# RWKV attention, Sinkhorn gate and eight experts on one core: the gate's products with x streaming past padded weights on four quarters of the array, and Sinkhorn's column sums over tiles by VectorE first

## The chip, the core and the metric

The kernel runs on one NeuronCore of a Trainium2 chip. The metric is the device time of one execution in microseconds (us). The program uses TensorE (matrix products; called PE in the profile, PEld for its weight loads), VectorE (DVE), ScalarE (ACT), GpSimd (POOL) and the DMA queues of SyncE (SP) and POOL. Each engine takes its instructions in the order in which the program gives them; semaphores order the engines against one another.

## The reference

The first half is a linear attention with a decaying state (batch 4, 8 heads, 768 steps, head size 48). Its output, turned into 3072 rows of 384 numbers, is `x`. The second half sends every row through eight experts and weighs their outputs with a matrix `P`, which Sinkhorn normalisation makes from the gate's logits:

```python
logits = x @ w_gate                      # 3072 x 8
P = np.exp(logits - logits.max())
for _ in range(8):
    P /= P.sum(1, keepdims=True) + 1e-09 # rows: over the 8 experts
    P /= P.sum(0, keepdims=True) + 1e-09 # columns: over all 3072 rows
    P *= N / E
for e in range(E):
    out += P[:, e:e+1] * (np.maximum(x @ w1[e], 0) @ w2[e])
```

## The kernel before, in words

The 3072 rows are 24 tiles of 128 (`NTT`). In every tile `x` is held transposed and as the sum of a high and a low fp16 part, in `hbx`: three chunks (`KC`) of 128 columns each, high and low.

**Attention loop.** A loop over `i` from 0 to 26 (`NTT + 3` passes) builds the tiles; tile `i - 2` is transposed by a DMA in pass `i`. Between its steps the loop calls `work(n)`, which emits the next `n` units of expert 0 from the list `units`: a unit `ph` (`g1_unit`) is 9 products into a bank `ph`, which ACT leaves with a Relu to `hb` and DVE then with the low part of the same values, also to `hb` (the DVE row SCALAR_TENSOR_TENSOR `hb<-ph,hb`); a unit `po` (`g2_half`) is 12 products into a bank `po`. There are two banks `ph`, and two of the pool `po`. The units come in groups of seven: ph po ph po ph po ph.

**Gate.** From pass 14 on, each pass also emits `gate_product` for up to two tiles: `x` is the stationary operand (128 columns), the gate's weights stream past it (16 columns, high and low, then 8), six products a tile into a bank `px`. ACT scales the result into `lparts`. In all there are 144 such products and 24 ACT exits.

**Ticks.** After the loop the remaining units are emitted one per tick: `for f in ticks.pop(tick)` runs the tick's small jobs, then `whole(units.pop(0))` emits one unit. The jobs are the last token combinations (`xv`), the weights of the next stage (`wms`, `ws`), and one step of the generator `sinkhorn()` at each of sixteen ticks. A step of Sinkhorn is what stands between two `yield`: a row step (DVE alone) or a column step. Before the change the column step is

```python
T.matmul(pc, ones, pm)          # TensorE: 192 columns, sums over the 128 partitions
V.tensor_reduce(cs, pc)         # DVE: over the 24 tiles
V.tensor_scalar(cs, cs, ...); V.reciprocal(cs, cs); V.tensor_tensor(pm, pm, cs)
```

Six column steps fall in the ticks 7, 12, 17, 22, 27 and 32. In each tick the Sinkhorn step is emitted before the other jobs, and the tick's unit last.

**Stages.** Then fourteen stages follow, one for each half of the experts 1 to 7. `g1_slots` emits slots of three products into banks `bA` to `bC`, `bY`, `bZ`, and after each slot four or five products of the rest of the stage before. The last two column steps stand in slots 5 and 13 of the first stage.

All order comes from the program's text: a product that is emitted ahead of another on TensorE also runs ahead of it.

Of the kernel before, what the change touches and what calls it, by code (L numbers as in the profile page):

```python
# [8 lines left out]
F32 = mybir.dt.float32  # L9
F16 = mybir.dt.float16  # L10
BF16 = mybir.dt.bfloat16
I32 = mybir.dt.int32
AF = mybir.ActivationFunctionType
# [20 lines left out]
def rwkv_sinkhorn_moe(  # L34
# [20 lines left out]
    P = 128  # L55
# [51 lines left out]
    def xpos(p0, n):  # L107
        return part(hbx, F16, p0 * TH * PX, (n * TH, 2 * KC, P)).rearrange("p (o t) c q -> p o c t q", t=TH)
# [4 lines left out]
    def xall(t, lo):  # L113
        return xtile(t)[:, lo * KC : (lo + 1) * KC, :]
# [385 lines left out]
    iswg = const.tile([P, 1], F32, name="iswg")  # L500
    swg = ac.tile([P, 1], F32, name="swg")
    wgm = ac.tile([P, 1], F32, name="wgm")
    wgp = ac.tile([P, KC, 2, E], F16, name="wgp")
    wgh, wgl = wgp[:, :, 0], wgp[:, :, 1]

    wga = ac.tile([P, KC, E], BF16, name="wga")
    gsum = []

    def gate_magnitude():
        S_.activation(wga, wg, AF.Abs, scale=1.0 / 1024)  # L510

    def gate_sums():
        gsum.append(ps2.tile([P, TB], F32, tag="po", name="pcs_g")[:, :E])
# [3 lines left out]
    def gate_split():  # L517
        V.tensor_reduce(wgm, gsum[0], axis=AX.X, op=ALU.max)
        pow2_scale(wgm, iswg, swg, 1.0)
        S_.activation(wgh, wg, AF.Copy, scale=swg)  # L520
        V.scalar_tensor_tensor(wgl, wg, swg, wgh, op0=ALU.mult, op1=ALU.subtract)

    st = {}

# [178 lines left out]
                T.transpose(pt[:, c * P : (c + 1) * P], xs[:, lo, c * P : (c + 1) * P], ident16)  # L703
            S_.copy(xall(tt, lo).rearrange("p c q -> p (c q)"), pt[:, : KC * P])

    gated = [0]

    def gate_product(tt, pg):
        for c in range(KC):
            xh_, xl_ = xall(tt, 0)[:, c, :], xall(tt, 1)[:, c, :]  # L710

            T.matmul(
                pg, xh_, wgp[:, c].rearrange("p l e -> p (l e)"), start=(c == 0), stop=False,
                skip_group_check=True,
            )
            T.matmul(
                pg[:, :E], xl_, wgh[:, c, :], start=False, stop=(c == KC - 1), skip_group_check=True
            )

    def gate_exit(tt, pg):  # L720
        S_.activation(
            lparts[:, tt].rearrange("p l e -> p (l e)"), pg, AF.Copy, scale=inv_s[:, tt : tt + 1]
        )
        del st[tt]


    TS = TB // 2
    xvs = [xv0]
# [89 lines left out]
    def work(n, hold=False):  # L818
        held[0] = hold
        for _ in range(n):  # L820
            if units:
                whole(units.pop(0))
        held[0] = False
# [43 lines left out]
    hooks[12, "early"] = [gate_magnitude]  # L867
    hooks[13, "early"] = [gate_sums]
    hooks[13, "middle"] = [gate_split]

    prep(0)
    load_part(4, "r", r)
# [18 lines left out]
    for i in range(NTT + 3):  # L891
        if i + 2 < NTT and i != TH + 1:
            prep(i + 2)
        if i > NE:
            send_x(i)
        leave(0)
        if i + 1 < NTT:
            bonus_dot(i + 1)
        if i + 1 < NTT and i:
            stage_b(i + 1)  # L900
        if 1 <= i <= NE:
            addends(i - 1)
        if i <= NE:
            send_x(i)
        n = i + 5 if i < 2 else i + 4
        if i != 2 and n < NTT:
            load_part(n, "r", r)
            load_part(n, "k", k)
        if i < 2:
            load_part(i + 3, "v", v)  # L910
        if i == 2:
            Q.dma_start(wg, w_gate.rearrange("(c p) e -> p c e", p=P))
        run(i, "loads")
        if NE <= i < NTT:
            bonus(i)
        leave(1)
        run(i, "early")
        if i > 10:
            work(1)
        if i < NTT:  # L920
            stage_c(i)
        run(i, "masked")
        if 1 <= i <= NTT:
            state_part(i - 1)
            scores_part(i - 1)
        if i == TH + 1:
            turn_x(TH - 1)
        if i < NTT:
            state_product(i)
        if 1 <= i <= NTT:  # L930
            sum_x(i - 1)
        if i < NTT:
            state_sum(i)
        if 1 <= i <= NTT:
            bound_x(i - 1)
        if i > NTT:
            work(2)
        run(i, "middle")
        if 1 <= i and i + 4 < NTT:
            load_part(i + 4, "v", v)  # L940
        for _ in range(n_steps(i)[0]):
            prepare()
        if i > 13:
            bank_ = ps2.tile([P, TB], F32, tag="po", name=f"px_{i}")
            todo = list(range(gated[0], min(gated[0] + 2, i - 2)))
            for n, tt in enumerate(todo):
                gate_product(tt, bank_[:, n * 2 * E : (n + 1) * 2 * E])
            for n, tt in enumerate(todo):
                gate_exit(tt, bank_[:, n * 2 * E : (n + 1) * 2 * E])
            gated[0] += len(todo)  # L950
        if i <= NTT:
            if i > TH:
                work(1 if i == 4 else 3 if i == 10 else 2, hold=i < 10)
            elif i == 0:
                S_.copy(onesb, ones)
                S_.copy(ident16, ident)
        run(i, "end")
        for _ in range(n_steps(i)[1]):
            prepare()
        if i == TH:  # L960
            prep(i + 3)
            scale_x(TH - 1)
            run(i, "last")
            units += [g1_unit(0, fc, 0) for fc in range(FHC)]
            units += [g2_half(0, t, 0, 0) for t in range(TH)]
        done = i - 2
        if TH <= done < NTT and done % TH == TH - 1:
            po_ = done // TH
            for p_, j in ((1, 0), (0, 1), (1, 1)) if po_ == 1 else ((po_, 0), (po_, 1)):
                turn[0] += 1  # L970
                g1 = [g1_unit(p_, fc, turn[0]) for fc in range(j * FHC, (j + 1) * FHC)]
                units += merged(g1, [g2_half(*a_) for a_ in pend])
                pend = [(p_, t, j, turn[0]) for t in range(TH)]
    assert not side and not hooks and not exits[0] and not exits[1]
    att.close()

# [94 lines left out]
    def sinkhorn():  # L1071
# [10 lines left out]
        for it in range(8):  # L1082
            rs = sm.tile([P, NTT], F32, tag="rs", name=f"rs_{it}")
            V.tensor_reduce(rs, pm, axis=AX.X, op=ALU.add)
            V.tensor_scalar_add(rs, rs, 1e-9)
            V.reciprocal(rs, rs)
            V.tensor_tensor(pm, pm, rs.unsqueeze(2).broadcast_to([P, NTT, E]), op=ALU.mult)
            yield
            pc = skp[0].tile([P, NTT, E], F32, tag=skp[1], name=f"pc_{it}")
            T.matmul(  # L1090
                pc.rearrange("p t e -> p (t e)"), ones, pm.rearrange("p t e -> p (t e)"),
                start=True, stop=True,
            )
            cs = sm.tile([P, E], F32, tag="cs", name=f"cs_{it}")
            V.tensor_reduce(cs, pc.rearrange("p t e -> p e t"), axis=AX.X, op=ALU.add)
            V.tensor_scalar(cs, cs, 1e-9, E / NT, op0=ALU.add, op1=ALU.mult)
            V.reciprocal(cs, cs)
            V.tensor_tensor(pm, pm, cs.unsqueeze(1).broadcast_to([P, NTT, E]), op=ALU.mult)
            yield
# [323 lines left out]
```

## Time and profile before

| | before |
|---|---|
| median of 3 runs | 1518.65 us (1518.31 to 1519.0) |
| the profiled execution | 1517.31 us |
| its span in the trace | 1515.8 us |
| TensorE busy | 1499.4 us (99%) |
| DVE, ACT, POOL busy | 1009.2, 675.9, 583.4 us |
| granted TensorE clock | 1.0 |

The difference of 1.5 us between the profiled execution and its span lies around the first and the last instruction. A row of the timeline has the start in us, the time from the first start to the last end of the instructions merged in it, the engine, the operation, the tile written and those read, the shape, the count, and in brackets the idle time of the engine before it with what ended it. Products of TensorE overlap: the end of one lies past the start of the next, so what one of them costs is the distance between starts, and the row of n products of d us each that spans w us has starts (w - d) / (n - 1) apart.

### The profile page before, as it was taken

Reading aid. Unit: us, or ns where it says so; the run is one execution under the profiler, and the core shown is the slowest. Engines: PE = TensorE matmul, PEld = TensorE weight load, DVE = VectorE, ACT = ScalarE, POOL = GpSimd, SP = SyncE. Lnnn points to the kernel's source line nnn. Section 1 sums busy time; section 2 is a strip of 40 time slices with the busy share of each in tenths; the row PEclk is TensorE's granted clock in tenths of the full one; section 3 lists DMA queues with packets and bytes.
Section 4 is the critical chain, followed back from the end, with each engine's and each line's share of the span. In section 5 each row is a group of like instructions: output and inputs, shape, how many; then the busy total and the mean of one; then the engine's idle time right before and its main releaser. Section 6 shows DMA issues by size and latency. Waiting matters only on the chain.

```text
span 1515.8 us, 29018 instructions
## 1 busy us (share of the span) xinstructions
PE 1499.4 (99%) x11734; PEld 849.2 (56%) x11734; DVE 1009.2 (67%) x1678; ACT 675.9 (45%) x1222; POOL 583.4 (38%) x685
## 2 busy tenths in 40 slices
PE   8999999999999999999999999999999999999999
PEld 6667765555555555555555555555555555555555
DVE  7898869576566666666676666666565666566464
ACT  6444435335353544545354544444353544445320
POOL 8779966200224243252424234242424233242200
PEclk9999999999999999999999999999999999999999
DMA  8765522211254666657656676655555455555433
GB/s 180 165 119 116 105 75 88 84 41 61 95 109 55 91 127 92 117 84 131 93 81 116 91 129 92 115 62 96 60 95 57 60 99 57 99 59 96 58 94 131
DMA packets 186441, 143.10 MB, mean 94 GB/s; under 512 B 108737, under 2 KB 180162, under 8 KB 186306
## 3 DMA queue, kind: packets, MB, share of 16 engines
q0 software_dynamic: 44928, 61.36, 32.8%
q1 hardware_dynamic: 141168, 79.87, 20.3%
q8 instruction: 92, 1.51, 0.4%
q14 instruction: 43, 0.35, 0.1%
q10 hardware_dynamic: 210, 0.00, 0.0%
HBM read 55.39 MB, written 80.23 MB: 89 GB/s over the span
## 4 chain that ended last, share of the span: by engine, by line
PE 93%; DVE 3%; issue 1%; ACT 0%; DVEq 0%
PE po L30 49%; PE bZ L30 12%; PE bY L30 12%; PE ph L30 5%; PE bA L30 5%; PE bB L30 5%; PE bC L30 2%; PE py L30 2%; PE pA L30 1%; PE prT L30 0%; PE pkT L30 0%; DVE hb L30 0%; PE px L30 0%; DVE ws L30 0%; DVE tb L30 0%
## 5 line engine op out<-in xcount | busy, mean ns | idle before, releaser
L30 PE MATMUL po<-ws,hbx 128*128 128x384 f16 x3360 | 736.8, 326 | 0.0
L30 POOL DMA_DIRECT2D accd<-stg x288 | 249.8, 868 | 694.5 <-ACT stg L30 676.0
L30 PEld LDWEIGHTS <-hbx 128*128 128x128 f16 x3504 | 333.5, 98 | 293.1 <-issue 1.0
L30 PEld LDWEIGHTS <-ws 128*128 128x128 f16 x3096 | 301.5, 98 | 246.8 <-issue 2.9
L30 ACT ACTIVATE hbx<-tb 128x512 f16<-128x512 f32 x224 | 141.0, 630 | 452.3 <-DVE tb L30 452.3
L30 PE MATMUL po<-ws,hb 128*128 128x384 f16 x1248 | 323.0, 326 | 0.1
L30 DVE TENSOR_TENSOR tb<-bY,tb 128x512 f32<-128x512 f32 x168 | 116.1, 691 | 176.5 <-PE bY L30 176.4
L30 ACT ACTIVATE stg<-po,pe 128x384 f32<-128x384 f32 x312 | 178.8, 573 | 122.3 <-PE po L30 97.9
L30 PE MATMUL bZ<-xv,ws 128*128 128x512 f16 x840 | 227.0, 379 | 0.5 <-DVE tb L30 0.4
L30 PE MATMUL bY<-xv,ws 128*128 128x512 f16 x840 | 227.0, 379 | 0.0
L30 DVE TENSOR_TENSOR tb<-bZ,tb 128x512 f32<-128x512 f32 x168 | 115.6, 688 | 135.8 <-PE bZ L30 135.8
L30 PEld LDWEIGHTS <-hb 128*128 128x128 f16 x1248 | 121.4, 98 | 93.4 <-DVE hb L30 0.4
L30 POOL TENSOR_TENSOR ucb<-rawb 128x256 f32<-128x256 f32 x84 | 75.7, 951 | 119.1 <-DMA rawb<-in_moe_w_dram 119.1
L30 DVE TENSOR_TENSOR tb<-bB,tb 128x512 f32<-128x512 f32 x112 | 77.4, 691 | 49.1 <-PE bB L30 47.2
L30 PE MATMUL ph<-hbx,ws 128*128 128x384 f16 x576 | 104.0, 326 | 1.7 <-DVE hb L30 0.9
L30 DVE SCALAR_TENSOR_TENSOR hb<-tb,hbx 128x512 f16<-128x512 f32 x112 | 77.1, 689 | 24.6 <-ACT hbx L30 19.5
L30 PE MATMUL bA<-xv,ws 128*128 128x512 f16 x336 | 90.8, 379 | 0.0
L30 PE MATMUL bB<-xv,ws 128*128 128x512 f16 x336 | 90.8, 379 | 0.0
L30 DVE SCALAR_TENSOR_TENSOR hbx<-tb,hbx 128x512 f16<-128x512 f32 x112 | 78.1, 698 | 14.7 <-ACT hbx L30 10.4
L30 ACT COPY tb<-bZ 128x512 f32<-128x512 f32 x56 | 32.7, 585 | 65.5 <-PE bZ L30 65.5
L30 DVE SCALAR_TENSOR_TENSOR hb<-ph,hb 128x384 f16<-128x384 f32 x64 | 34.9, 551 | 28.7 <-ACT hb L30 28.4
L30 DVE TENSOR_REDUCE wms<-rawb 128x1 f32<-128x768 f32 x56 | 51.7, 943 | 0.0
(175 smaller groups left out, 1471.5 us busy)
## 6 DMA issues: line engine op xcount, KB each, us to landing
accd<-stg POOLq DMA_DIRECT2D x288, 192.0 KB, 3.7
rawb<-in_moe_w_dram SPq DMA_DIRECT2D x28, 768.0 KB, 7.9
e0d<-stg SPq DMA_DIRECT2D x48, 192.0 KB, 2.0
hb<-e0d SPq DMA_DIRECT2D x48, 192.0 KB, 3.6
vn<-in_v_dram SPq DMA_DIRECT2D x24, 192.0 KB, 3.9
accd<-stg SPq DMA_DIRECT2D x24, 192.0 KB, 1.8
accd<-hb POOLq DMA_DIRECT2D x24, 192.0 KB, 4.8
rawb<-accd SPq DMA_DIRECT2D x24, 192.0 KB, 2.4
```

Of the source, the lines that this page charges most:

```text
L30: return lambda *a, **k: self.tc.keep_in_program_order(f(*a, **k))
```

## The change

**The gate.** `wgp` is padded with zeros to 32 columns (`QP`) for each chunk and part. Now the padded weights are stationary and `x` streams: one product takes three tiles (384 columns) and writes 32 partitions of a bank `pg`; four of them, for four groups of three tiles, write the four quarters of the partitions. Twelve tiles take 24 products. The bank holds the logits turned; ACT copies it to a tile `stg_g` (`gate_products`), and three transposes on TensorE and one multiplication by DVE bring it into `lparts` (`gate_turn`). The first twelve tiles are done in pass 15, the others in pass 26, whose transposes come after two more units `work(2)`; so the ticks begin two units later in the list than before.

**Sinkhorn.** In the column step DVE first sums `pm` over the 24 tiles into `cs` (128 x 8), TensorE then sums `cs` over the partitions (8 columns in place of 192), and DVE reads the result. The steps stand at the same ticks and slots.

```diff
-    wgp = ac.tile([P, KC, 2, E], F16, name="wgp")
-    wgh, wgl = wgp[:, :, 0], wgp[:, :, 1]
+    wgp = ac.tile([P, KC, 2, QP], F16, name="wgp")
+    wgh, wgl = wgp[:, :, 0, :E], wgp[:, :, 0, E : 2 * E]
...
     def gate_magnitude():
         S_.activation(wga, wg, AF.Abs, scale=1.0 / 1024)
+        S_.copy(wgp.rearrange("p c l e -> p (c l e)"), zeros[:, : KC * 2 * QP])
...
         V.scalar_tensor_tensor(wgl, wg, swg, wgh, op0=ALU.mult, op1=ALU.subtract)
+        S_.copy(wgp[:, :, 1, :E], wgh)
...
-    def gate_product(tt, pg):
-        for c in range(KC):
-            xh_, xl_ = xall(tt, 0)[:, c, :], xall(tt, 1)[:, c, :]
-
-            T.matmul(
-                pg, xh_, wgp[:, c].rearrange("p l e -> p (l e)"), start=(c == 0), stop=False,
-                skip_group_check=True,
-            )
-            T.matmul(
-                pg[:, :E], xl_, wgh[:, c, :], start=False, stop=(c == KC - 1), skip_group_check=True
-            )
-
-    def gate_exit(tt, pg):
-        S_.activation(
-            lparts[:, tt].rearrange("p l e -> p (l e)"), pg, AF.Copy, scale=inv_s[:, tt : tt + 1]
-        )
+    GP = P // QP
+    gated = {}
+
+    def gate_products(b):
+        pg = ps2.tile([P, TB], F32, tag="po", name=f"pg_{b}")[:, : TH * P]
+        for c in range(KC):
+            for lo in range(2):
+                for g in range(GP):
+                    T.matmul(
+                        pg[g * QP : (g + 1) * QP].rearrange("p (t q) -> p t q", q=P),
+                        wgp[:, c, lo], xpos(b * GP + g, 1)[:, 0, lo * KC + c],
+                        start=(c + lo == 0), stop=(c + lo == KC), skip_group_check=True,
+                    )
+        gated[b] = stgp.tile([P, DM], F32, tag="stg", name=f"stg_g{b}")
+        S_.copy(gated[b], pg)
+
+    def gate_turn(b):
+        pt = ps2.tile([P, TB], F32, tag="po", name=f"pgT_{b}")[:, : TH * P]
+        for t in range(TH):
+            T.transpose(pt[:, t * P : (t + 1) * P], gated[b][:, t * P : (t + 1) * P], ident)
+        n = GP * TH
+        V.tensor_tensor(lparts ..., pt ..., inv_s ..., op=ALU.mult)
...
+    hooks[15, "middle"] = [lambda: gate_products(0)]
+    hooks[16, "early"] = [lambda: gate_turn(0)]
+    hooks[NTT + 2, "middle"] = [lambda: gate_products(1)]
...
-        if i > 13:
-            bank_ = ps2.tile([P, TB], F32, tag="po", name=f"px_{i}")
-            todo = list(range(gated[0], min(gated[0] + 2, i - 2)))
-            for n, tt in enumerate(todo):
-                gate_product(tt, bank_[:, n * 2 * E : (n + 1) * 2 * E])
-            for n, tt in enumerate(todo):
-                gate_exit(tt, bank_[:, n * 2 * E : (n + 1) * 2 * E])
-            gated[0] += len(todo)
...
+    work(2)
+    gate_turn(1)
...
-            pc = skp[0].tile([P, NTT, E], F32, tag=skp[1], name=f"pc_{it}")
-            T.matmul(
-                pc.rearrange("p t e -> p (t e)"), ones, pm.rearrange("p t e -> p (t e)"),
-                start=True, stop=True,
-            )
             cs = sm.tile([P, E], F32, tag="cs", name=f"cs_{it}")
-            V.tensor_reduce(cs, pc.rearrange("p t e -> p e t"), axis=AX.X, op=ALU.add)
-            V.tensor_scalar(cs, cs, 1e-9, E / NT, op0=ALU.add, op1=ALU.mult)
+            V.tensor_reduce(cs, pm.rearrange("p t e -> p e t"), axis=AX.X, op=ALU.add)
+            pc = skp[0].tile([P, TB], F32, tag=skp[1], name=f"pc_{it}")[:, :E]
+            T.matmul(pc, ones, cs, start=True, stop=True)
+            V.tensor_scalar(cs, pc, 1e-9, E / NT, op0=ALU.add, op1=ALU.mult)
```

Three places in the order of the instructions follow; names carry the tile's number, and what an instruction waits for stands in brackets.

DVE at the second column step (tick 12), before. `xv` is a token combination's low part, `wms` and `wmas` are maxima of the next weights, `hb<-ph` is the low exit of a unit `ph`:

```order
L30 TENSOR_TENSOR xv_4481<-tb,xv_4481 128x3x256 [waits Activation_49]
L30 TENSOR_REDUCE wms_4488<-rawb 128x1
L30 TENSOR_REDUCE wmas_4489<-wms_4488 128x2 [waits DVE_49]
L30 SCALAR_TENSOR_TENSOR hb_73<-ph_3_4721,hb_73 128x384 [waits Activation_49]
L30 TENSOR_REDUCE cs_4735<-pc_4733 128x8 [waits PE_49]
L30 TENSOR_SCALAR cs_4735<-cs_4735 128x8 [waits DVE_49]
```

The same place on DVE in the change:

```order
L30 SCALAR_TENSOR_TENSOR hb_73<-ph_4_4613,hb_73 128x384 [waits Activation_49]
L30 TENSOR_TENSOR xv_4394<-tb,xv_4394 128x3x256 [waits Pool_49]
L30 TENSOR_REDUCE wms_4401<-rawb 128x1
L30 TENSOR_REDUCE wmas_4402<-wms_4401 128x2 [waits DVE_49]
L30 TENSOR_REDUCE cs_4646<-pm 128x8
L30 TENSOR_SCALAR cs_4646<-pc_4648 128x8 [waits PE_49]
```

The sum over tiles keeps its place behind the jobs of the tick before, but it no longer reads `pc`: it makes what `pc` is made from.

TensorE around the column steps 2 to 6 in the change:

```order
L30 MATMUL po_0_4630<-ws_75,hb_73 128x384
L30 MATMUL pc_4648<-cs_4646,ones 128x8 [waits DVE_49]
...
L30 MATMUL ph_7_4733<-hbx,ws_75 128x384
L30 MATMUL pc_4747<-cs_4745,ones 128x8 [waits DVE_49]
...
L30 MATMUL ph_2_4824<-hbx,ws_75 128x384
L30 MATMUL pc_4838<-cs_4836,ones 128x8 [waits DVE_49]
...
L30 MATMUL ph_5_4913<-hbx,ws_75 128x384
L30 MATMUL pc_4927<-cs_4925,ones 128x8 [waits DVE_49]
...
L30 MATMUL ph_0_4993<-hbx,ws_75 128x384
L30 MATMUL pc_5007<-cs_5005,ones 128x8 [waits DVE_49]
```

Before, the product read `pm`, written by DVE in the row step three ticks earlier, and the steps 2 to 5 stood behind a `ph`, 1 and 6 behind a `po`; now 1 and 2 stand behind a `po` and 3 to 6 behind a `ph`, since the ticks begin two units later.

TensorE at the second half of the gate (pass 26 and after it) in the change:

```order
L30 MATMUL po_0_4308<-ws_75,hb_73 128x384
L30 LDWEIGHTS wgp
L30 MATMUL pg_4324<-hbx,wgp 32x384
...
L30 MATMUL ph_5_4351<-hbx,ws_75 128x384
...
L30 MATMUL po_0_4363<-ws_75,hb_73 128x384
L30 MATMUL pgT_4379<-ident,stg_g_4349 128x128 x3
```

The last two groups of `px` before, six products each, stood between the units of the passes 25 and 26; now 24 products `pg` stand in pass 26 in one piece, with one `ph` and one `po` between them and the transposes.

More of the change, by code (lines that the diff above doesn't have):

```diff
@@ L704, in turn_x @@
             S_.copy(xall(tt, lo).rearrange("p c q -> p (c q)"), pt[:, : KC * P])
-    gated = [0]
-    def gate_product(tt, pg):
+    GP = P // QP
+    gated = {}
+    def gate_products(b):
+        pg = ps2.tile([P, TB], F32, tag="po", name=f"pg_{b}")[:, : TH * P]
         for c in range(KC):
-            xh_, xl_ = xall(tt, 0)[:, c, :], xall(tt, 1)[:, c, :]
-            T.matmul(
-                pg, xh_, wgp[:, c].rearrange("p l e -> p (l e)"), start=(c == 0), stop=False,
-                skip_group_check=True,
-            )
-            T.matmul(
-                pg[:, :E], xl_, wgh[:, c, :], start=False, stop=(c == KC - 1), skip_group_check=True
-            )
-    def gate_exit(tt, pg):
-        S_.activation(
-            lparts[:, tt].rearrange("p l e -> p (l e)"), pg, AF.Copy, scale=inv_s[:, tt : tt + 1]
+            for lo in range(2):
[12 more added lines that the diff above has]
+        n = GP * TH
+        V.tensor_tensor(
+            lparts[:, b * n : (b + 1) * n].rearrange("p (g t) l e -> p g t (l e)", t=TH),
+            pt.rearrange("p (t g e) -> p g t e", t=TH, g=GP)[:, :, :, : 2 * E],
+            inv_s[:, b * n : (b + 1) * n].rearrange("p (g t) -> p g t", t=TH)
+            .unsqueeze(3).broadcast_to([P, GP, TH, 2 * E]),
+            op=ALU.mult,
         )
-        del st[tt]
     TS = TB // 2
```

## The prediction

> **What bounds the kernel now.** I read the page first, then TensorE's waits, then the timeline around the gate and around Sinkhorn's column steps.
>
> ```profile
> PE 1499.4 (99%) x11734; PEld 849.2 (56%) x11734; DVE 1009.2 (67%) x1678; ACT 675.9 (45%) x1222; POOL 583.4 (38%) x685
> PE 93%; DVE 3%; issue 1%; ACT 0%; DVEq 0%
> PE py L30 <- ACT rT L30: 2.1, 2, 1.7
> ...
> PE px L30 <- issue: 0.9, 1, 0.9
> ...
> PE bZ L30 <- DVE tb L30: 0.4, 1, 0.4
> ```
>
> The first row is the page's busy time, the second the engines' shares of the chain that ended last, the others are rows of TensorE's waits (total, times, longest). TensorE is busy from end to end and carries 93% of the chain. So a change is worth what it takes out of TensorE's stream, and costs what it makes TensorE wait. A saving on DVE or ACT is worth nothing by itself. But "99% busy" also says that TensorE hardly ever waits for DVE, and that is what the Sinkhorn edit touches.
>
> **The gate's products.** The timeline of TensorE, with the old products between two neighbours, and the transposes of another tile:
>
> ```profile
> 117.06 0.60 PE L30 MATMUL prT<-ident,rp 128*128 128x128 f32 x4
> 117.49 0.60 PE L30 MATMUL pkT<-ident,kp 128*128 128x128 f32 x4
> ...
> 122.16 0.52 PE L30 MATMUL py<-vn,kp 128*32 128x48 f32 x32
> 122.62 0.46 PE L30 MATMUL px<-wgp,hbx 128*128 128x16 f16 x12
> 122.93 2.27 PE L30 MATMUL ph<-hbx,ws 128*128 128x384 f16 x13
> ```
>
> Removed: twelve `px` hold TensorE from 122.62 to 122.93, 0.31 us or 26 ns each; 144 of them cost 3.7 us. One of them also waited 0.9 us (the row of waits above), so at most 4.6 us goes away.
>
> Added: 48 `pg` with 384 streamed columns. Alone, a product of 384 columns has its starts (2.27 - 0.33) / 12 = 0.162 us apart (row `ph`; one takes 0.326). Whether four quarters run at once is seen in `py<-vn,kp`, which also writes 32 columns of the array at a time: its starts are (0.52 - 0.21) / 31 = 10 ns apart (one takes 0.207), four in 0.040 us. A product of 192 fp32 columns has its starts 0.163 apart (the row `pc` x2 further down: 0.49 less 0.326), so 48 columns alone need 0.041. Four quarters thus take the time of one, with two different streams among the four here. I take 12 x 0.162 = 1.95 us; in turn it would be 48 x 0.162 = 7.8.
>
> The Trainium skill (TensorE: Matmul & The Clock Gate, Part 3) gives 3.07 times for four packed tiles in one measurement; by that the twelve rounds would cost an estimated 0.6 us more. The `py` row shows the whole factor of four, and the row decides.
>
> Further: six transposes at (117.49 - 117.06) / 4 = 0.109, 0.65 us, and a change of the array's split ahead of and behind the second half. Ahead of `px` one such change shows: the last `py` starts at 122.47 and would be followed at 122.51; `px` starts at 122.62. So two times 0.1. The first half follows `py` in the same split and needs none more than before. The sum is 1.95 + 0.65 + 0.2 = 2.8 us.
>
> The gain is thus 3.7 - 2.8 = 0.9 us if the 0.9 us of wait turns up elsewhere, 1.8 if it is gone. I take 1.5. The rest of the edit (24 exits of ACT become two copies; one zero fill, one copy, two multiplications of DVE) lies beside TensorE: the transposes come a `ph` and a `po` after the copy, 3.4 us, for one copy of about 0.5 us.
>
> **Sinkhorn's column step.** On TensorE the product of 192 columns gives way to one of 8. The nearest rows are a product with one column, which also waited for DVE:
>
> ```profile
> 226.35 0.20 DVE L30 TENSOR_SCALAR md_gm<-ident,mt_gm 1x1 f32<-1x1 f32 x1
> ...
> 226.66 0.38 PE L30 MATMUL pmax_gm<-md_gm,ones 1*128 1x1 f32 x2
> 226.97 0.82 PE L30 MATMUL ph<-hbx,ws 128*128 128x384 f16 x4
> ```
>
> It holds TensorE 0.31 us, as long as the present `pc` (0.33, from 235.27 to 235.60 below): the fp32 weights `ones` are loaded twice either way. So the smaller product saves nothing. It starts 0.1 us after DVE's end (226.55), which is the price of the hand-over.
>
> On DVE the sum over tiles stays (0.35 us). What changes is who waits. Now TensorE does `pc` in passing, and DVE reads it when it gets there. After the change TensorE must wait until DVE has got there and summed. Behind the waiting `pc` on TensorE stands the whole next unit. So the loss of a step is the time by which DVE's sum lags behind TensorE's arrival. The old rows show that lag, since `cs<-pc` stands at the same place in DVE's order. First the step after tick 7, then the second:
>
> ```profile
> 234.78 0.55 DVE L30 SCALAR_TENSOR_TENSOR hb<-ph,hb 128x384 f16<-128x384 f32 x1
> 235.27 0.49 PE L30 MATMUL pc<-pm,ones 128*128 128x192 f32 x2
> 235.60 1.63 PE L30 MATMUL ph<-hbx,ws 128*128 128x384 f16 x9
> 236.19 0.72 DVE L30 TENSOR_SCALAR cs<-cs 128x8 f32<-128x8 f32 x1
> ...
> 243.88 0.49 PE L30 MATMUL pc<-pm,ones 128*128 128x192 f32 x2
> 245.32 1.62 PE L30 MATMUL ph<-hbx,ws 128*128 128x384 f16 x9 [0.95 <-DVE hb L30]
> 246.78 2.11 PE L30 MATMUL po<-ws,hb 128*128 128x384 f16 x12
> ...
> 247.60 0.16 DVE L30 TENSOR_REDUCE wmas<-wms 128x2 f32<-128x4 f32 x1
> 247.68 0.55 DVE L30 SCALAR_TENSOR_TENSOR hb<-ph,hb 128x384 f16<-128x384 f32 x1
> 248.14 0.35 DVE L30 TENSOR_REDUCE cs<-pc 128x8 f32<-128x192 f32 x1
> ...
> 235.30:249.00 13.70, 12.75 (x79) 7.78 (x79) 12.93 (x22) 5.58 (x11) 13.07 (x17) 1.00 0.13 44
> ```
>
> (The last row is a stretch's busy time: length, PE, PEld, DVE, ACT, POOL.)
>
> Step 1: DVE is free at 235.33, the sum ends at 235.68, TensorE gets it at 235.78 instead of 235.27: 0.5 us.
>
> Step 2: DVE is full here (12.93 of 13.7 us) and gets to its sum 4.3 us after TensorE's `pc`. In the new order DVE has the same work between the two sums, 248.14 - 236.19 = 11.95 us, and TensorE three `ph` (9 x 0.162 = 1.46) and two `po` (12 x 0.162 = 1.95) and the product itself, 8.28 + 0.31 = 8.6 us. DVE starts on its stretch about 0.45 us after TensorE's `pc` begins (hand-over and product). So TensorE waits 0.45 + 11.95 + 0.35 + 0.1 - 8.6 = 4.25 us. Of it, 1.1 us is lost already (245.32 less 243.88 less 0.33, the bracket's wait, for a bank `ph` that DVE gives back). The next unit finds its bank free now, so the step costs 3.15 us more. After it DVE has caught up.
>
> Steps 3 to 6 stand right behind a `ph` in the new order. Then DVE must first bring out that unit's low part, which waits for ACT. The old fifth step shows the chain:
>
> ```profile
> 271.36 0.49 PE L30 MATMUL pc<-pm,ones 128*128 128x192 f32 x2
> 271.56 0.49 ACT L30 ACTIVATE hb<-ph 128x384 f16<-128x384 f32 x1 [0.97 <-PE ph L30]
> 272.08 0.56 DVE L30 SCALAR_TENSOR_TENSOR hb<-ph,hb 128x384 f16<-128x384 f32 x1
> 272.55 0.35 DVE L30 TENSOR_REDUCE cs<-pc 128x8 f32<-128x192 f32 x1
> ```
>
> From TensorE's arrival at 271.36 to the sum's end, 272.90, and 0.1 for the hand-over: 1.64 us, four times, 6.55 us. No other DVE job stands between, so this holds even with DVE idle before.
>
> Steps 7 and 8, in slots 5 and 13 of the first stage:
>
> ```profile
> 296.85 0.49 PE L30 MATMUL pc<-pm,ones 128*128 128x192 f32 x2
> 298.75 0.34 DVE L30 TENSOR_REDUCE cs<-pc 128x8 f32<-128x192 f32 x1
> ...
> 309.47 0.49 PE L30 MATMUL pc<-pm,ones 128*128 128x192 f32 x2
> 312.13 0.35 DVE L30 TENSOR_REDUCE cs<-pc 128x8 f32<-128x192 f32 x1
> ```
>
> By the same sum 299.09 + 0.1 - 296.85 = 2.35 us and 312.48 + 0.1 - 309.47 = 3.1 us. The slots' order does not change, and DVE's work there hangs on TensorE's, so both shift together.
>
> All eight: 0.5 + 3.15 + 6.55 + 2.35 + 3.1 = 15.65 us. Bounds: steps 3 to 6 could cost nothing (then 9.1), and nothing of the rest excludes the whole sum; a gain of TensorE is excluded, because the product costs the same. Little can be won back: behind step 2 TensorE now waits once, 0.4 us (`bZ`, in the rows of waits).
>
> **Sum.** 15.65 - 1.5 = 14.15 us. The profiled execution would go from 1517.31 (span 1515.8 and 1.5 around it) to 1531.5. The median before lies 1.3 us above the profiled execution, so the forecast is 1518.65 + 14.15 = 1532.8 us.
>
> **Rivals.**
>
> *The lag costs only where DVE is truly behind.* If a unit's low exit came out in time in the steps 3 to 6, 9.1 - 1.5 = 7.6 us would be left: 1526.2. Against it stands the order, in which the exit is ahead of the sum.
>
> *The quarters run in turn.* Then the gate costs 5.85 us more: 1538.6. The `py` row speaks against it, though its four quarters share two streams and the new ones have four.
>
> *TensorE's clock falls in the longest wait.* The start of the trace shows TensorE slower after idling:
>
> ```profile
> L30 PE MATMUL pz<-zeros x19: 379/631/631, 1.5 to 9.1; 128*128 128x512 f16 x19
> 1.52 5.92 PE L30 MATMUL pz<-zeros 128*128 128x512 f16 x15 [1.52 <-DVE zeros L30]
> ```
>
> The first fifteen start (5.92 - 0.63) / 14 = 0.378 us apart; at 379 ns each, 0.216 apart as in the full-speed rows of the same shape, they would save 2.3 us. A wait of 4.25 us, in step 2, may bring that once: 1535.1. The longest wait of TensorE now is 1.7 us (the row `py`), so the trace cannot say where it sets in. The Trainium skill (TensorE: Matmul & The Clock Gate, Part 1) says that a whole free-running window of about 3.4 us without work brings half the clock; no run here shows it yet.
>
> *TensorE does not stop.* If it ran the unit behind a waiting `pc`, as it would have to for the edit to be free, only the gate's 1.5 to 1.8 us would be left: 1517.0, on the other side. It decides at the first `pc` that DVE reaches late. Against it: at 245.32 TensorE waited 0.95 us for DVE, with products behind in its queue.
>
> **Chances.** Forecast 0.74, low exit in time 0.08, quarters in turn 0.05, clock 0.05, no stop 0.08. With this measurement about 0.2% (3 us) can be told from no change. Slower by more: the first four cases, 0.92. The last case would be faster by 1.7 us, within 0.2%; with the spread of the gate's gain (up to 4.6 us if the turned products cost nothing) I put 0.04 on faster and 0.04 on the same. The range from 1525.5 to 1538 takes in the smaller loss and the clock, and stops short of the quarters in turn.
>
> **What would show it.** Right: in the timeline each `pc` starts about 0.1 us after the end of `cs<-pm`, and TensorE's waits get a row `pc <- DVE cs` of about 16 us in eight times; `pg` starts in fours 0.162 us apart. Wrong: no such row (TensorE did not stop); `pg` products 0.16 us apart one by one; `ph` products over 0.33 us behind the second step (the clock).

## The result, and the profile after

The changed kernel takes 1534.35 us in the median of five executions (1533.8 to 1537.27), beside 1518.31 us (1516.37 to 1519.0) for the kernel before in the same series. So the change costs 16.0 us by the medians. The ratio, which goes by all executions, is 1.0113, with a 95% interval from 1.01 to 1.0125, or 17.1 us between the means. The forecast was 1532.8, in a range from 1525.5 to 1538.

The profiled execution of the changed kernel took 1535.28 us; its span is 1533.8 and its granted clock 0.997, where it was 1.0 before. The page and TensorE's waits, for comparison with the first fence of the prediction:

```profile
PE 1503.2 (98%) x11644; PEld 848.6 (55%) x11644; DVE 1011.4 (66%) x1680; ACT 672.1 (44%) x1202; POOL 582.3 (38%) x685
PE 94%; DVE 3%; ACT 1%; issue 1%; POOL 1%; ACTq 0%; DVEq 0%; POOLq 0%
PE pc L30 <- DVE cs L30: 13.6, 8, 2.6
PE py L30 <- issue: 6.2, 5, 1.6
...
PE po L30 <- issue: 0.3, 1, 0.3
```

The third row is new. TensorE waits eight times for DVE's sum, 13.6 us in all, and the longest wait is 2.6. It has 90 products fewer than before, and yet 3.8 us more of busy time: a first sign that some products ran slowly. The last two rows, waits that nothing in the trace ends ("issue"), are taken up further down.

**Sinkhorn's steps in the timeline.** Step 2 of the column sums, the one that stands in DVE's densest stretch:

```profile
241.50 0.39 PE L30 MATMUL pc<-cs,ones 128*128 128x8 f32 x2 [0.74 <-DVE cs L30]
241.75 0.97 PE L30 MATMUL ph<-hbx,ws 128*128 128x384 f16 x5
241.93 0.17 DVE L30 TENSOR_SCALAR cs<-pc 128x8 f32<-128x8 f32 x1 [0.48 <-PE pc L30]
...
250.27 0.34 PE L30 MATMUL po<-ws,hb 128*128 128x384 f16 x1 [0.24 <-DVE hb L30]
...
252.62 0.49 DVE L30 TENSOR_REDUCE cs<-pm 128x8 f32<-128x192 f32 x1
253.17 0.39 PE L30 MATMUL pc<-cs,ones 128*128 128x8 f32 x2 [2.56 <-DVE cs L30]
253.41 2.26 PE L30 MATMUL ph<-hbx,ws 128*128 128x384 f16 x9
```

The sum ends at 253.11, and `pc` starts at 253.17. TensorE stands for 2.56 us, with the next `ph` ready behind it. The product itself holds TensorE 0.24 us (253.17 to 253.41); the one of 192 columns held it 0.33. The nine `ph` behind it start (2.26 - 0.33) / 8 = 0.24 us apart instead of 0.162.

A wait in brackets counts from the end of the product before, which comes 0.16 us after the point at which the next one would have started; so each wait costs its bracket and 0.16. By step, for TensorE:

| column step | bracket (us) | cost (us) | forecast |
|---|---|---|---|
| 1 | 0.74 | 0.9 | 0.5 |
| 2, with the 0.24 at 250.27 | 2.56 + 0.24 | 3.1 | 4.25 |
| 3 to 6, each | 1.57 | 1.74 | 1.64 |
| 7 | 2.12 | 2.3 | 2.35 |
| 8 | 1.90 | 2.1 | 3.1 |

Together that is 15.3 before rounding. To be taken off are the waits of before that are gone (1.1 at step 2; 0.44 + 0.16 at a `bZ` 0.64 us ahead of step 8, and 0.2 at an earlier `bZ`, a delay too short for a bracket) and the shorter product (8 x 0.08 = 0.6): about 12.8 us remain.

**The clock.** Busy times of stretches of 3.41 us in the loop and around the steps 2 and 7 (length, PE, PEld, DVE, ACT, POOL, granted clock, DMA share, GB/s):

```profile
49.44:52.85 3.41, 1.61 (x53) 1.25 (x56) 3.31 (x8) 2.66 (x6) 2.44 (x2) 1.00 0.99 267
52.85:56.27 3.42, 3.42 (x123) 2.85 (x116) 3.32 (x9) 1.06 (x1) 2.75 (x3) 0.50 0.95 170
...
247.41:250.83 3.42, 2.96 (x18) 1.46 (x15) 3.42 (x6) 1.25 (x3) 3.34 (x5) 1.00 0.00 0
250.83:254.24 3.41, 1.07 (x8) 0.75 (x9) 2.83 (x7) 1.07 (x2) 3.25 (x5) 1.00 0.17 60
254.24:257.65 3.41, 3.41 (x12) 1.62 (x11) 1.92 (x3) 0.49 (x1) 3.41 (x6) 0.50 0.00 0
257.65:261.07 3.42, 3.42 (x23) 2.06 (x22) 2.60 (x8) 1.91 (x3) 1.80 (x2) 1.00 0.16 57
...
308.86:312.27 3.41, 1.29 (x8) 0.55 (x7) 3.04 (x5) 1.00 (x2) 3.25 (x5) 1.00 0.14 52
312.27:315.68 3.41, 3.41 (x12) 1.57 (x13) 1.33 (x4) 0.00 (x0) 3.41 (x5) 0.50 0.11 41
...
326.00:329.34 3.34, 1.76 (x11) 1.11 (x12) 2.16 (x6) 0.33 (x1) 0.00 (x0) 1.00 0.00 0
```

Behind the steps 2 and 7 the granted clock is 0.50 for one stretch, then full again. In the slow stretch behind step 2 TensorE works on 12 products; in the next one, at full clock, on 23. In the kernel with all sums early (a run further down), which has full clock there, the same units take 1.7 us less. That is so behind both steps, 3.3 us together before rounding. The last row is step 8, whose wait is 1.90 us; the clock is full behind it too (no further stretch of half clock follows).

So the Sinkhorn edit costs 12.8 + 3.3 = 16.1 us in this execution. From the last `py` of the attention loop to the end it takes 16.9 us more than before (209.64 to 1533.79, before 208.53 to 1515.83), so about 0.8 of that is left for the second half of the gate, and 1.1 us lies in the loop. The sum, 18.0, is that of two single executions, one 1.0 us below its median and one 0.9 above.

The clock has a part in that spread. The first two rows show a stretch of half clock in the loop, behind a wait of TensorE for ACT; the profiled execution of the kernel before has none there (its granted clock is 1.0). One such stretch takes 0.5 x 3.41 / 1518 = 0.0011 off the mean clock. In the three series below, the kernel before had a granted clock of 1.0 in 28 executions and of 0.999 in 51 of 83; their medians are 1516.6 and 1518.0 us. The five executions of the change have 0.995 to 0.998.

**The gate.** The two halves:

```profile
131.29 1.28 PE L30 MATMUL pg<-hbx,wgp 128*32 128x384 f16 x24
132.51 1.64 PE L30 MATMUL ph<-hbx,ws 128*128 128x384 f16 x9
...
223.53 1.16 PE L30 MATMUL pg<-hbx,wgp 128*32 128x384 f16 x24
224.62 1.64 PE L30 MATMUL ph<-hbx,ws 128*128 128x384 f16 x9
...
228.04 0.49 PE L30 MATMUL pgT<-ident,stg_g 128*128 128x128 f32 x3
228.37 1.63 PE L30 MATMUL ph<-hbx,ws 128*128 128x384 f16 x9
```

The halves hold TensorE 1.22 and 1.09 us, the three transposes 0.33. That is 2.97 us for both, with the change of the split behind them, against 2.8 forecast and 3.7 for the products that are gone. TensorE's own work became shorter, then, by 0.7 us. But the kernel did not: the next section shows it.

### The profile page after: what moved, and what is told of

Read it like the earlier page. It is cut to its first block, busy times and chain, and to the rows that moved or that the text cites. A ratio compares the mean times of both kernels' runs of the same rounds, so it can differ in the third digit from the quotient of the medians.

```text
span 1533.8 us, 28815 instructions
## 1 busy us (share of the span) xinstructions
PE 1503.2 (98%) x11644; PEld 848.6 (55%) x11644; DVE 1011.4 (66%) x1680; ACT 672.1 (44%) x1202; POOL 582.3 (38%) x685
## 4 chain that ended last, share of the span: by engine, by line
PE 94%; DVE 3%; ACT 1%; issue 1%; POOL 1%; ACTq 0%; DVEq 0%; POOLq 0%
PE po L30 48%; PE bY L30 12%; PE bZ L30 12%; PE ph L30 5%; PE bA L30 5%; PE bB L30 5%; PE py L30 3%; PE bC L30 2%; PE pA L30 1%; DVE hb L30 1%; PE pkT L30 1%; PE prT L30 1%; ACT hb L30 0%; ACT hbx L30 0%; DVE xv L30 0%
## 5 line engine op out<-in xcount | busy, mean ns | idle before, releaser
L30 PEld LDWEIGHTS <-hbx 128*128 128x128 f16 x3360 | 328.8, 98 | 291.2
L30 ACT ACTIVATE hb<-ph 128x384 f16<-128x384 f32 x64 | 31.0, 488 | 65.0 <-PE ph L30 64.4
```

What stands on the lines that cost most here:

```text
L30: return lambda *a, **k: self.tc.keep_in_program_order(f(*a, **k))
```

## The experiments

In each series the kernel before ran on the same chip; its medians there were 1517.67, 1517.72 and 1517.68 us. Times below are medians of 4 to 12 executions, and the code cuts are shortened. One kernel's executions lie up to 5.5 us apart, so intervals are given where it matters.

### Each part alone

The change's gate with the old column step (`e1`):

```diff
+            T.matmul(pc, ones, pm)                 # 192 columns, as before
-            V.tensor_reduce(cs, pm, axis=AX.X)
-            T.matmul(pc, ones, cs)
+            V.tensor_reduce(cs, pc, axis=AX.X)
```

> The gate as in the change, Sinkhorn's column step as before. The forecast's sum says 1.5 us faster than before (0.9 to 1.8). The rival, from the trace of the change, in which the first ph behind the gate's last transposes starts 1.9 us later than before: TensorE's work in the attention loop is not what sets the loop's length, so the products saved there are worth little, and the second half of the gate stands outside of that cover: 0 to 2 us slower. Neither of them gives any row pc <- DVE cs in TensorE's waits.

The old gate with the change's column step, the same edit the other way round (`e2`):

> The gate as before, Sinkhorn's column step as in the change. If TensorE's wait for DVE's sum is the whole cause: 12 to 15 us slower. In this order the steps 2 to 5 stand behind a ph and 1 and 6 behind a po, so step 6 should wait for nothing (about 1.6 us less than in the change) and steps 3, 4, 5 for 1.6 us of idle time each. If the two parts of the change disturb each other (the ticks that begin two units later), it is well under 12 us.

The gate alone took 1519.36 us, a ratio of 1.0014 (1.0005 to 1.0023): it costs 1.7 us, where the prediction had it gain 1.5. Sinkhorn's edit alone took 1530.6 us, 1.0091 (1.0076 to 1.0106), or 12.9 us more. Its waits:

```profile
PE pc L30 <- DVE cs L30: 12.1, 7, 3.0
PE py L30 <- issue: 3.3, 3, 1.5
PE px L30 <- issue: 1.1, 1, 1.1
```

There are seven waits, since the ticks begin two units earlier without the change of the gate and step 6 stands behind a `po`, where its sum is in time. In its profiled execution the clock falls once at the column steps, behind step 7; the longest wait, 2.96 us at step 2, has none behind it. The two parts alone cost 12.9 + 1.7 = 14.6 us; together they cost step 6's 1.74 us as well, since the new gate moves the ticks by two units. That makes 16.3, against 16.0 measured.

### The column steps in pieces

If the loss is TensorE's wait for a sum that DVE makes late, the sum must be made earlier, at the end of the row step ahead of it. This is the change with only that (`e3` all eight, `e5` the second alone, `e6` the third to sixth):

```diff
+            if it in range(8):          # e5: (1,)   e6: (2, 3, 4, 5)
+                V.tensor_reduce(cs, pm, axis=AX.X)
             yield
-            V.tensor_reduce(cs, pm, axis=AX.X)
+            if it not in range(8):
+                V.tensor_reduce(cs, pm, axis=AX.X)
             T.matmul(pc, ones, cs)
```

> The change, but DVE's sum over tiles is issued at the end of the row step, three ticks ahead of the product that reads it. The same instructions on each engine, only this one moved. If the lag of the sum is the cause, all eight waits go, and the time is that of the gate part alone less 0.7 us (the product of 8 columns holds TensorE 0.24 us in the trace, the old one 0.33): 1516 to 1520. If the smaller product itself, or the new read of pc by DVE, cost the time, it stays above 1530.

> The change, with the sum over tiles of the second column step alone issued at the end of its row step. In the trace of the change TensorE lost 3.1 us to this wait (5.08 from the first product of the po ahead to pc, less 1.95), of which the kernel before lost 1.1 too, in another place; and behind it the granted clock was 0.5 for 3.4 us, which cost 1.7 us (ph 2.06 in place of 1.46, po 3.03 in place of 1.95). If the wait brings the slow clock: no stretch of clock 0.5 behind this step, and 3.6 us less than the change, 1530.7. If the slow clock has another cause and comes anyway: 1.9 us less, 1532.4, and the stretch stays.

> The change, with the sums of the column steps 3 to 6 alone issued at the end of their row steps. If each of these waits is the low exit of the ph ahead and the sum behind it (1.74 us each in the trace of the change): 7.0 us less than the change, 1527.4, with the waits of the steps 2, 7 and 8 as they were. If TensorE only waits for something else instead, such as a bank: less than 4 us are won.

| kernel | us | ratio to before | against the change | waits of `pc` for `cs` |
|---|---|---|---|---|
| the change | 1534.35 | 1.0113 | | 13.6 us, 8 times |
| all eight early | 1517.24 | 0.9998 (0.9989 to 1.0007) | -17.1 | none |
| the second early | 1529.98 | 1.0086 (1.0073 to 1.01) | -4.4 | 11.2 us, 7 times |
| the third to sixth early | 1527.32 | 1.0065 (1.0052 to 1.0079) | -7.0 | 7.9 us, 4 times |

The fourth column compares medians of different series; with each kernel taken against the kernel before of its own series, the three differences are 16.5, 3.8 and 6.4 us. With all eight sums early no wait of `pc` is left, and the whole loss is gone. The four middle steps are worth 7.0 us, 4 x 1.74 by the table above. The second is worth 4.4: its wait costs 2.7 us by the table (2.56 and 0.16), and the rest fits the slow stretch behind it, which that kernel doesn't have:

```profile
251.00:255.00 4.00, 4.00 (x27) 2.42 (x25) 3.90 (x9) 2.15 (x5) 3.84 (x5) 1.00 0.14 51
255.00:259.00 4.00, 4.00 (x27) 2.36 (x25) 3.68 (x8) 1.79 (x3) 4.00 (x5) 1.00 0.14 49
...
309.00:313.00 4.00, 4.00 (x23) 2.15 (x22) 2.73 (x5) 1.50 (x3) 3.08 (x5) 1.00 0.02 4
```

The clock is 1.00 where the change had 0.50, with the same work around it. The kernel with the third to sixth early keeps step 2's wait of 2.56 us, and the slow stretch stands behind it again (253.05 to 256.46 us). So the rival "TensorE's clock falls in the longest wait" came true at this step, beside the forecast's own mechanism, as far as single executions show it. But the last row lies behind step 7, which still waits 2.1 us here, and no slow stretch followed it. Not every wait of that length brings one: the 2.96 us of Sinkhorn's edit alone brought none either.

### What the gate's products were worth

The kernel before without its 144 products and 24 exits (`e4`; it leaves the gate out, so that its logits are zero):

```diff
+    V.memset(lparts, 0.0)
-            bank_ = ps2.tile([P, TB], F32, tag="po", name=f"px_{i}")
-                gate_product(tt, bank_[...])
-                gate_exit(tt, bank_[...])
```

> Before, without the gate's 144 products and its 24 exits; the logits are zeros, so P is uniform, and the rest of the computation is unchanged. It shows what TensorE time in the attention loop is worth. If TensorE sets the loop's length: 3.7 us of products and the 0.9 us wait fall away, 4 to 4.6 us faster. If something else sets it: under 2 us faster.

It took 1514.72 us, 0.9986 (0.9977 to 0.9995): 2.1 to 3 us less, where 4.6 had been put down as the most that could go (3.7 of work and 0.9 of wait). The wait of 0.9 us at a `px` is gone, but another stands somewhere else:

```profile
140.30 0.52 PE L30 MATMUL py<-vn,kp 128*32 128x48 f32 x32
140.76 0.50 PE L30 MATMUL po<-ws,hb 128*128 128x384 f16 x2
142.39 0.81 PE L30 MATMUL po<-ws,hb 128*128 128x384 f16 x4 [1.14 <-issue]
```

So that wait didn't belong to the gate's products. Something else makes TensorE stand, and it comes back at another product.

The quarters one after another, in the gate-only kernel (`e7`):

```diff
-        for c in range(KC):
-            for lo in range(2):
-                for g in range(GP):
+        for g in range(GP):
+            for c in range(KC):
+                for lo in range(2):
```

> The kernel with the gate part alone, its 24 products of each half issued one quarter after the other (six for one quarter, then six for the next) in place of four quarters side by side. If the quarters run at once in the change and cannot here: each half holds TensorE 24 x 0.162 = 3.9 us in place of 1.0, and the time rises by 2.9 us if the attention loop covers the first half, by 5.8 us if not: 1522 to 1525. If the quarters never ran at once, nothing changes.

```profile
131.22 2.16 PE L30 MATMUL pg<-hbx,wgp 128*32 128x384 f16 x24
133.31 0.99 PE L30 MATMUL ph<-hbx,ws 128*128 128x384 f16 x5
```

A half then holds TensorE 2.09 us, 0.9 to 1.0 more than in the change's order, and the kernel takes 1520.78 us, 1.0022 (1.0013 to 1.0031), less than was expected of it. 24 products in turn would be 24 x 0.162 = 3.9 us. In the trace the 24 starts can be read as four runs of six, 0.162 us apart within a run, which begin at 131.218, 131.549, 131.891 and 132.232 us. By that reading each quarter begins 0.34 us after the one before, while it still runs, so TensorE overlaps quarters even in this order. The change's order does better: in its second half the last of six rounds starts 1.16 - 0.33 = 0.83 us after the first, five steps of 0.166, so four quarters take the time of one.

### The waits that nothing ends

The "issue" waits of more than 0.2 us in the attention loop were then counted by their place in TensorE's stream: the number of weight loads, products and semaphore instructions ahead of each.

| kernel | start of the waiting product (us) and remainder of its number by 256 |
|---|---|
| before | 32.37: 170; 38.13: 170; 70.67: 171; 106.49: 171; 185.61: 170 |
| the change | 32.62: 170; 38.38: 170; 71.55: 171; 159.96: 170; 178.35: 170; 195.82: 170 |
| the change, all sums early | 31.86: 169; 38.17: 169; 70.73: 169; 158.95: 168; 194.14: 168 |
| before without gate products | 32.12: 169; 38.70: 169; 71.95: 169; 107.56: 169; 142.39: 168 |

All stand at the same place in a block of 256. The part of the page on DMA queues (packets, MB, share) has, for the change:

```profile
q8 instruction: 91, 1.49, 0.4%
```

Each of the 91 packets brings 16384 bytes, and TensorE's 23376 instructions are 91.3 blocks of 256. The transfer behind the wait at 158.95 started at 156.5, that behind 185.61 at 182.9: 2.5 and 2.7 us ahead. A wait appears where TensorE comes to the boundary sooner than that after the transfer's start. This is mostly so where it runs through a block fast, above all in the products `py`, which start 10 ns apart; but the wait at 38.13 ends a block that took 4.7 us without it, since its transfer started only at 35.59. What decides when a transfer starts was not found. The theory is therefore that the next part of the program is late. It says that a shift of the stream moves the waits to other products. Four kernels test it: all sums early, with 36, 68 or 100 small products in place of four large ones ahead of the loop (32, 64 or 96 more, `e9` to `e11`), and the old gate with 64 more (`e12`, from `e8` of the next part):

```diff
-    spin(4)
+    pz16 = ps2.tile([P, TB], F32, tag="po", name="pz16")
+    for _ in range(36):                 # 68, 100
+        T.matmul(pz16[:, : 2 * E], zeros[:, :P], zeros[:, : 2 * E])
```

> This is the change with its sums over tiles early (whose time was 1517.24 us), with 32 products more ahead of the attention loop: 36 products of 16 columns of zeros take the place of four of 512 columns, in a stretch in which TensorE waits 0.76 us for a transfer anyway. Theory (TensorE's code): TensorE waits where a dense run of products crosses a boundary of 256 instructions of its stream, because the next 16 KB of its code come in too late; so far all such waits stand at the instructions 168 to 171 of a 256. With 64 instructions more ahead they go to other products: those at 158.95 (1.15 us) and 194.14 (0.77 us) are gone, new ones stand near 100, 118 or 170 us, at the same remainder of the count. Time: 1516.2 to 1518.2 us, as the new places are about as dense. Rival (the waits belong to what the gate's edit does to the banks or the engines there): the two waits stay at the same products, and the time within 0.5 us of 1517.24.

> The same with 64 products (128 instructions) more. Theory (TensorE's code): the waits at 158.95 and 194.14 are gone, new ones near 126, 144 or 179 us; 1516.2 to 1518.2 us. Rival: the waits stay at the same products, and the time within 0.5 us of 1517.24.

> The same with 96 products (192 instructions) more. Theory (TensorE's code): the waits at 158.95 and 194.14 are gone; the boundaries then fall in the least dense places of the four alignments, near 108, 126 and 178 us, so the waits behind 90 us sum to under 1.2 us instead of 1.9, and the time is 0.5 to 1.5 us lower than with the other alignments: 1515.7 to 1516.7 us. Rival: the waits stay at the same products, and the time within 0.5 us of 1517.24 (or above it by the 0.3 us that the added products may cost).

> The old gate with Sinkhorn's new form and its sums early (whose time was 1515.51 us), with 64 products more ahead of the loop. Theory (TensorE's code): the wait of 0.4 to 0.9 us of a px product at 185.6 us is gone, a new one may stand near 128 or 190 us; the old gate has its time by its alignment as well, so it moves by 0.3 to 1.5 us to either side. Rival (the old gate has no waits by its nature): within 0.3 us of 1515.51.

The place of the wait at 158.95 us, without a shift and with 32 products more:

```profile
157.36 0.43 PE L30 MATMUL py<-vn,kp 128*32 128x48 f32 x22
158.95 0.33 PE L30 MATMUL py<-vn,kp 128*32 128x48 f32 x10 [1.15 <-issue]
159.21 1.64 PE L30 MATMUL ph<-hbx,ws 128*128 128x384 f16 x9
```

```profile
162.28 0.52 PE L30 MATMUL py<-vn,kp 128*32 128x48 f32 x32
162.74 1.64 PE L30 MATMUL ph<-hbx,ws 128*128 128x384 f16 x9
```

The 32 `py` now pass in one piece. In the four shifted kernels the waits stand at other products, a `pg` among them, and again at remainders from 165 to 170 (but for one of 0.2 us at a `pcs` in two of them). With 64 products more, a wait falls into the gate's first half:

```profile
134.11 0.50 PE L30 MATMUL pg<-hbx,wgp 128*32 128x384 f16 x7
136.43 0.97 PE L30 MATMUL pg<-hbx,wgp 128*32 128x384 f16 x17 [1.82 <-issue]
```

| all sums early | us | ratio (95%) | such waits behind 12 us, total |
|---|---|---|---|
| new gate, no shift | 1517.24 | 0.9998 (0.9989 to 1.0007) | 5.9 |
| 32 more | 1516.54 | 0.9989 (0.998 to 0.9998) | 4.8 |
| 64 more | 1520.41 | 1.002 (1.0011 to 1.0029) | 11.1 |
| 96 more | 1517.2 | 0.9999 (0.999 to 1.0008) | 5.8 |
| old gate, no shift | 1515.51 | 0.9984 (0.9975 to 0.9993) | 4.1 |
| old gate, 64 more | 1518.68 | 1.0004 (0.9995 to 1.0013) | 7.8 |

The theory held for where the waits stand. For the times it did less well: with 64 more both kernels became 3.2 us slower, more than was expected, and 96 more, expected as the fastest, was not. Still, the order of the times is that of the waits in the last column within either gate (1517.2 and 1517.24 can't be told apart), and the loop is where they differ: from the last `py` to the end the four kernels with the new gate take 1306.12 to 1306.18 us.

In three pairs that differ in the gate alone (gate alone against before; all sums early; both with 64 more) the new gate is 1.7 us slower by the medians each time; each of these differences is uncertain by about 1 us. In the profiles 0.8 to 1.1 of it lies behind the last `py` (with all sums early 1306.12 us there with the new gate, 1305.14 with the old one): a second half of 24 `pg` and three transposes (1.42 us) stands there in place of 24 `px` (0.62). In the loop TensorE has 1.55 us less to do with the new gate (24 `pg` and three transposes in place of 120 `px`). That work is gone, but the waits for code take it back. From the `py` at 122.42 us of the kernel before, the last one ahead of the gate's first products, to the last `py`:

| kernel | us | waits for code in it | without them |
|---|---|---|---|
| before | 86.11 | 0.9 | 85.2 |
| Sinkhorn's edit alone | 86.38 | 1.1 | 85.3 |
| old gate, all sums early | 86.33 | 0.8 | 85.5 |
| before without gate products | 83.82 | 1.1 | 82.7 |
| gate alone | 86.10 | 2.1 | 84.0 |
| the change | 86.92 | 2.9 | 84.0 |
| new gate, all sums early | 85.96 | 1.9 | 84.0 |

Without the waits the new gate's loop is 1.2 to 1.5 us shorter; with them it is from 0.4 shorter to 0.8 longer. These are single executions. Loop and end together make 0.6 to 1.1 us in the first two pairs' profiles; the rest of the 1.7 us was not located.

### The best version

The old gate with the change's column step and all sums early (`e8`):

```diff
-            T.matmul(pc, ones, pm)                 # 192 columns, behind the yield
+            V.tensor_reduce(cs, pm, axis=AX.X)     # ahead of the yield
             yield
-            V.tensor_reduce(cs, pc, axis=AX.X)
+            T.matmul(pc, ones, cs)                 # 8 columns
```

> The gate as before; Sinkhorn's column step as in the change, but with the sum over tiles issued at the end of the row step. No wait pc <- DVE cs. The product of 8 columns holds TensorE 0.24 us in place of 0.33, eight times, so 0.7 us faster than before if TensorE's time is all that counts here: 1516.5 to 1518. If the early sum on DVE makes the low exits late, 1 to 2 us slower.

It takes 1515.51 us, 0.9984 (0.9975 to 0.9993), 2.2 us less than before and less than both kernels, and more of a gain than the 0.7 us expected. Two column steps, the first and the second:

```profile
235.43 0.28 PE L30 MATMUL pc<-cs,ones 128*128 128x8 f32 x2
235.57 1.14 PE L30 MATMUL ph<-hbx,ws 128*128 128x384 f16 x6
...
243.85 0.28 PE L30 MATMUL pc<-cs,ones 128*128 128x8 f32 x2
244.60 1.62 PE L30 MATMUL ph<-hbx,ws 128*128 128x384 f16 x9 [0.46 <-DVE hb L30]
```

Where the small product did not wait, it holds TensorE only 0.14 us (235.43 to 235.57), not the 0.24 of the change and not 0.33; eight times, that saves 1.5 us. Step 2 also gets shorter, as DVE reads 8 numbers there instead of 192 ahead of the exit that a `ph` waits for: the wait there was 0.95 us and is 0.46 now. Together that is 2.0 us. In the profiles the whole difference lies in this part: from the last `py` to the end this kernel takes 1305.14 us and the kernel before 1307.29, 2.15 more, while the loop is 0.2 us longer. So by these profiles the gain is not one of the code's alignment, though a shift by 64 products costs the same kernel 3.2 us by the medians.

## Why the prediction was right or wrong

**Right: the mechanism and the size of the Sinkhorn loss.** TensorE stops at `pc`, eight times, and waits for DVE's sum. The row foretold as "about 16 us in eight times" reads 13.6 us in eight. Removing the lateness removes 17.1 us (16.5 within its own series), so the rival "TensorE does not stop" falls, and so does "the low exit in time": steps 3 to 6 cost 7.0 us by experiment, against 6.55.

**Mis-sized, in both directions.** Step 2 was put at 4.25 us and took 3.1: DVE's stretch between the two sums was 252.62 - 241.93 = 10.7 us, not the 11.95 of the old order. It held the same jobs, but three of them spanned less: the first operation on `cs` 0.17 instead of 0.72, the multiplication of `pm` 0.36 instead of 0.60, the last `xv` 1.05 instead of 1.52. Step 8 took 2.1 instead of 3.1, and step 1 took 0.9 instead of 0.5. Steps 3 to 6 took 0.1 us more each, because the sum over `pm` takes 0.49 us where the sum over `pc` took 0.35; the forecast had left the duration as it was. "The smaller product saves nothing" was wrong: it holds TensorE 0.24 us instead of 0.33 where it has waited, and 0.14 where it has not, so the row with one column (0.31), which had waited, did not show it. Altogether the waits came out at 12.8 us instead of 15.65.

**A rival that came on top: the clock.** It was given 0.05, for step 2, at 2.3 us. It came twice at the column steps of the profiled execution, behind the steps 2 and 7, and cost 3.3 us. The forecast's own sum was therefore right partly by luck: 2.85 us too much in the waits, 3.3 too little in the clock.

**Wrong: the gate's gain of 1.5 us.** The step that failed is "the gain is thus 3.7 - 2.8 = 0.9 us if the 0.9 us of wait turns up elsewhere, 1.8 if it is gone". The work went about as computed (3.7 less 2.97). The wait does turn up elsewhere, and longer: such waits belong to the place in the program's code and not to the products, as the shifted kernels show, and from 122.42 us to the last `py` they come to 1.9 to 2.9 us with the new gate against 0.8 to 1.1 with the old one. That takes the 1.2 to 1.5 us which the loop does gain. The sum also did not ask where each half stands: the second one stands behind the loop, in place of 24 `px` only, and costs 0.8 us there. So the gate costs 1.7 us by the medians in three pairs, of which 0.6 to 1.1 is accounted for.

**Quarters.** They do run at once, 0.166 us a round in the second half and (1.28 - 0.33) / 5 = 0.19 in the first. The rival "in turn" falls, and even the order that should have shown it costs only 0.9 to 1.0 us a half. The Trainium skill's factor of 3.07 (TensorE: Matmul & The Clock Gate, Part 3) is measured there on four tiles packed by rows, while the quarters here are columns; the 0.6 us more that it gave is not borne out by these two rows.

So the forecast of +14.15 us met +16.0. Sinkhorn's 15.65 was about right (16.1 in the profiled execution; 12.9 + 1.74 = 14.6 by the medians), in other parts than it was made of; the miss is the sign of the gate.

## What to carry to other kernels

Where one engine works in order and is nearly always busy, a step that makes it wait for another engine costs that engine's lag behind it, whatever the step saves; read the lag from the old rows, and move the work that is waited for to an earlier place, which here removed the 16 us of loss, and with the old gate made it a gain of 2. A wait of 2 to 3 us can also bring a stretch of slow clock, 1.7 us here, but does not always. A change of 1 or 2 us in a dense stream is smaller than what a shift of the code alone does, so it needs a comparison over several alignments.

## What the runs showed of the hardware

**The clock falls without a whole idle window.** The stretches of 3.41 us ahead of the two slow ones are not empty: TensorE was busy for 1.07 and 1.29 us of them, and its waits were 2.56 and 2.12 us. The two slow stretches start 58.03 us apart, 17.0 times 3.413, and the one in the loop 201.39 us ahead of the first, 59.0 times, so they lie on one grid. A wait of 1.90 us, whose stretch on that grid (326.00 to 329.34 in the view, but for its first 0.08 us) had 1.76 us of work, brought none. The Trainium skill (TensorE: Matmul & The Clock Gate, Part 1) tells of a free-running window of 3413 ns and of half the clock after an idle one. The grid and the length agree with the trace; that the window must be idle does not, as one with 31%, one with 38% and, in the loop, one with 47% of work were followed by half the clock. Where the limit lies was not measured, and the share of work alone doesn't give it: in the kernel with Sinkhorn's edit alone, 44% ahead of 308.50 brought half the clock, while 45% ahead of 247.06 did not, nor 42% in the kernel with the third to sixth early (the rows below). In the last two cases the wait, of 2.96 and 2.51 us, ran on into the next stretch:

```profile
305.10:308.50 3.40, 1.51 (x10) 0.95 (x11) 2.75 (x6) 1.00 (x2) 3.32 (x6) 1.00 0.16 58
308.50:311.90 3.40, 3.40 (x11) 1.45 (x10) 1.45 (x3) 1.01 (x2) 2.83 (x4) 0.50 0.00 0
...
243.65:247.06 3.41, 1.52 (x10) 0.69 (x7) 3.38 (x6) 1.69 (x3) 3.33 (x4) 1.00 0.16 58
247.06:250.48 3.42, 2.35 (x15) 1.51 (x16) 2.31 (x6) 0.44 (x1) 3.26 (x6) 1.00 0.03 5
...
300.83:304.24 3.41, 1.43 (x8) 0.56 (x6) 3.04 (x5) 1.00 (x2) 3.25 (x5) 1.00 0.24 89
304.24:307.65 3.41, 2.88 (x17) 1.71 (x18) 2.37 (x6) 0.26 (x1) 3.41 (x5) 1.00 0.16 58
```

**Code is waited for.** TensorE stood for 0.2 to 2.8 us at places that lie 256 instructions apart, and went on 2.1 to 3.3 us after the transfer of 16 KB of its program had started. The Trainium skill (Runtime: NRT & Kernel Launch, Instruction fetch mechanics) names blocks of 16 KiB with 256 instructions, fetched while the one before runs, and calls the cost of a crossing mostly hidden. The size agrees. Hidden it is not here: 5.4 us of such waits stand in the kernel before, and shifting the code changes the median by up to 3.9 us.
